# Attention and a Mish feed-forward on one core: the keys' weights turned on TensorE, a shorter warm-up, and a new order of steps

## The chip, the cores and the metric

The kernel runs on one core of a Trainium2 chip. The metric is the time of one execution on the device, in microseconds (us). Three executions of the kernel before took 173.52, 173.74 and 173.78 us; the median is 173.74.

## What is computed

The input x (2048 tokens by 512) is normalised once. Two branches read it: a linear attention of 32 heads of 16, whose features are softmaxes of q and k after a small learned matrix w_phi, and a feed-forward of width 1792 with the Mish function. Their sum is added to x.

```python
def _A_ref(x, wqkv, w_phi, wo):
    qkv = (x @ wqkv).reshape(B, S, 3, H, Dh).transpose(2, 0, 3, 1, 4)
    q, k, v = qkv[0], qkv[1], qkv[2]
    pq = jnp.einsum("bhsd,hdf->bhsf", q, w_phi)
    pk = jnp.einsum("bhsd,hdf->bhsf", k, w_phi)
    phi_q = jnp.concatenate([_softmax(pq), _softmax(-pq)], axis=-1)
    phi_k = jnp.concatenate([_softmax(pk), _softmax(-pk)], axis=-1)
    kv = jnp.einsum("bhsf,bhsd->bhfd", phi_k, v)
    z  = jnp.einsum("bhsf->bhf", phi_k)
    num = jnp.einsum("bhqf,bhfd->bhqd", phi_q, kv)
    den = jnp.einsum("bhqf,bhf->bhq", phi_q, z)[..., None] + 1e-6
    return (num / den).transpose(0, 2, 1, 3).reshape(B, S, D) @ wo

def _B_ref(x, w1, b1, w2):
    h = jnp.einsum("bsd,df->bsf", x, w1) + b1
    return jnp.einsum("bsf,fd->bsd", h * jnp.tanh(softplus(h)), w2)

xn = _layernorm(x)
return x + _A_ref(xn, A_wqkv, A_w_phi, A_wo) + _B_ref(xn, B_w1, B_b1, B_w2)
```

## The kernel before

**Tiles.** The tokens are 16 tiles of 128, in four groups of four. A matrix product over the 512 input columns is four matmuls of 128 rows, one after the other in one PSUM bank. There are six banks of 512 columns, named by @0 to @5 in the list of steps, and a pair of banks (tag "kv") for the attention's sums.

**The order is written out by hand.** `STEPS` (lines 24 to 59) is a string of step names with their arguments; the loop at lines 623 to 625 calls one function for each. Each engine gets its instructions in the order in which the steps are called, and works through them in that order; waits between engines are put in from the data. A number behind @ is the bank that a step writes, and a step that writes a bank waits until the one before it in that bank has been read. The letters v and a at the end say whether VectorE (DVE) or ScalarE (ACT) does a copy or a reciprocal.

**The steps that matter here**, with the functions that they call:

- LS i, RS i, AZ i, TP i, TC i: the first four token tiles. LS takes mean and variance on DVE (lines 545 to 547), RS the inverse root on POOL in two instructions (174 to 177), AZ centres and scales on DVE, TP turns the tile with four transposes on TensorE against an identity, TC copies it from PSUM into `xnT`. LN g and AP g k do the same for the later groups, four tiles at a time, and turn by DMA on the SP queue (line 186).
- F0 kt and FD kt: w_phi is folded into the keys' weights ahead of use. `wT` holds the 512 columns of wqkv for the keys, turned; four matmuls (F0) with the block-diagonal `Wbd` (step WB, from the small load `wsrc`) give 128 rows of the folded weights, and FD copies them into `wkp`. F and FC do so for the queries, later, into the first half of `wqk`; the second half of that tile holds wo.
- LP: the logits of keys for token tiles 0 and 1, eight matmuls that take turns by `kt`. L s i: those of any other tile (s below 4 keys, s from 4 queries). WL 1 and WL 2: two of group 1 into the kv banks. LC copies logits to bf16.
- V t and VC t: values of a tile, and their copy into `vext`.
- H u, M u: 128 of the 1792 hidden columns for one group of tokens, and its Mish on ScalarE with the bias `b1f` (made by PB and CB from `b1b`). O t is the second layer of a tile (14 matmuls of 512 columns), P t adds the attention's output to it (4 matmuls), Y t adds x and stores. The last tile is cut in two, OH, PH and YH.
- E s l: largest (l = 0) or smallest (l = 1) logit of each 16, and the difference, on DVE. X s k: exponentials on ScalarE. S s k: their sums on DVE. R s k and N s k: reciprocal and product for keys; A g k: the sums over tokens on TensorE. W s k: the ratio for queries, and a turn by DMA on SP. KV masks the sums. Q h i, G h i, C h: numerators and denominators on TensorE, their copy from PSUM on ScalarE, and the division with a turn by DMA on SP.

**The start.** Ahead of the steps come the loads. On the SP queue: x_sb of tile 0, then the keys' weights as a turning DMA (`load_turned`, lines 140 to 144), then tiles 2 and 3, wv, half of w1, tiles 4 to 7, the rest of w1. On ScalarE's queue: wsrc, tile 1, b1b. ScalarE then loads the table of the Mish function. POOL makes the identity and the block mask. TensorE meanwhile runs `WARM` = 12 matmuls of ones (lines 511 to 516), whose result nobody reads. ScalarE's functions lie in two tables, one for Mish and one for exponential and logarithm; `table` (134 to 138) loads one when the other is active.

**Buffers.** The sums of exponentials `s` have three buffers, `log`, `r2` and `r` two each (pool `smx`).

Of the kernel before, what the change touches and what calls it, by code (L numbers as in the profile page):

```python
# [29 lines left out]
9; M 10; AP 1 1; H 11 @5; E 0 1; V 4 @1; X 0 1; WL 1; LN 2; V 6 @4; VC 4 a; X 0 0; L 1 0 @2; L 1 3  # L30
@0; LC 1 0 a; V 5 @3; LN 3; VC 5 a; H 12 @1; WL 2; H 13 @2; VC 6 a; S 0 0; LC 1 3 a; M 11; V 3 @3; M
12; M 13; H 14 @4; H 15 @0; H 16 @5; H 17 @1; VC 3 a; M 14; H 18 @2; M 15; M 16; M 17; LC 1 2 a; H
19 @3; AP 2 0; AP 2 1; AP 3 0; L 2 0 @4; LC 2 0 a; L 2 1 @0; LC 2 1 a; V 2 @5; S 0 1; L 2 2 @1; M
18; LC 1 1 a; M 19; H 20 @4; LC 2 2 a; AP 3 1; H 21 @0; WT; H 22 @2; M 20; VC 2 a; R 0 1 v; L 2 3
@3; H 23 @1; R 0 0 v; N 0 1; M 21; N 0 0; H 24 @4; M 22; LC 2 3 a; F 0 @5; F 1 @0; E 1 0; E 1 1; M
23; M 24; F 2 @2; E 2 0; E 2 1; FC 0 a; H 25 @3; H 26 @1; FC 1 a; H 27 @4; M 25; M 26; L 3 2 @5; FC
2 a; M 27; V 7 @0; L 3 3 @3; V 11 @1; F 3 @2; L 3 0 @4; LC 3 0 v; LC 3 2 a; L 3 1 @5; A 0 0; X 1 0;
X 1 1; A 0 1; LC 3 3 a; FC 3 v; S 1 0; V 8 @4; LC 3 1 a; VC 7 a; L 4 0 @2; E 3 0; VC 8 a; LC 4 0 a;
L 4 1 @3; LC 4 1 a; L 4 3 @5; VC 11 a; L 4 2 @0; X 2 0; V 9 @4; L 5 0 @2; H 28 @3; H 29 @1; VC 9 a;
LC 4 2 v; M 28; M 29; H 30 @0; H 31 @4; H 32 @3; M 30; H 33 @1; H 34 @0; M 31; M 32; M 33; M 34; H  # L40
35 @4; M 35; H 36 @3; M 36; S 1 1; LC 4 3 a; R 1 0 v; E 3 1; LC 5 0 a; N 1 0; R 1 1 v; H 37 @1; H 38
@0; H 39 @4; H 40 @3; H 41 @5; H 42 @2; S 2 0; A 1 0; M 37; N 1 1; M 38; M 39; M 40; A 1 1; M 41; M
42; X 3 0; L 6 3 @1; L 5 2 @0; V 10 @4; VC 10 a; L 5 1 @3; LC 5 2 a; L 6 0 @5; E 4 0; E 4 1; X 2 1;
S 3 0; V 15 @2; VC 15 a; V 13 @4; VC 13 a; LC 6 0 a; R 2 0 a; S 2 1; DW 3; R 3 0 a; X 3 1; L 6 1 @0;
LC 5 1 a; DW 2; N 3 0; N 2 0; L 5 3 @2; O 0 @4; S 3 1; V 12 @5; V 14 @3; LC 6 1 a; LC 5 3 a; O 1 @0;
L 6 2 @2; R 2 1 a; N 2 1; VC 14 a; LC 6 3 a; VC 12 v; R 3 1 a; N 3 1; X 4 0; A 2 0; S 4 0; LC 6 2 a;
A 2 1; A 3 0; W 4 0 v; X 4 1; H 43 @3; M 43; A 3 1; H 44 @1; H 45 @5; M 44; H 46 @2; M 45; H 47 @3;
M 46; M 47; H 48 @1; KV; H 49 @5; H 50 @2; Q 0 0; M 48; M 49; G 0 0; M 50; H 51 @3; H 52 @1; H 53
@5; S 4 1; W 4 1 v; M 51; M 52; H 54 @2; H 55 @3; Q 0 1; M 53; E 5 0; E 5 1; M 54; E 6 0; L 7 0 @1;
M 55; G 0 1; C 0 a; X 5 0; LC 7 0 a; L 7 1 @5; X 5 1; O 2 @2; O 3 @3; LC 7 1 a; L 7 2 @1; LC 7 2 a;  # L50
S 5 0; Q 1 0; L 7 3 @5; G 1 0; E 6 1; W 5 0 a; P 0; P 1; Y 0; Q 1 1; O 4 @1; G 1 1; LC 7 3 a; O 5
@4; S 5 1; Q 2 0; O 6 @5; C 1 a; P 2; G 2 0; W 5 1 v; Y 1; Q 2 1; P 3; O 7 @0; E 7 0; X 6 0; S 6 0;
G 2 1; Q 3 0; C 2 a; G 3 0; Y 2; Y 3; X 6 1; O 8 @2; Q 3 1; W 6 0 v; E 7 1; S 6 1; P 4; P 5; G 3 1;
C 3 a; Q 4 0; X 7 0; Y 4; W 6 1 v; X 7 1; S 7 0; O 9 @3; O 10 @1; G 4 0; Q 4 1; P 6; P 7; G 4 1; Y
5; Y 6; C 4 a; Q 5 0; W 7 0 a; G 5 0; O 11 @4; Q 5 1; Y 7; O 12 @5; S 7 1; G 5 1; C 5 a; Q 6 0; G 6
0; O 13 @0; Q 6 1; G 6 1; W 7 1 v; P 8; P 9; Q 7 0; C 6 a; G 7 0; P 10; P 11; Y 8; Q 7 1; G 7 1; O
14 @2; Y 9; Y 10; C 7 a; P 12; P 13; OH 0 @3; PH 0; Y 11; P 14; OH 1 @1; PH 1; Y 12; Y 13; YH 0; Y
14; YH 1
"""
# [3 lines left out]
def kernel(  # L63
# [76 lines left out]
    def load_turned(base_col):  # L140

        wT = lnp.tile([P, 4, 512], BF16, name="wT", tag="xn")
        nc.sync.dma_start_transpose(out=wT[:], in_=A_wqkv[:, base_col : base_col + D])
        return wT

# [343 lines left out]
    nc.sync.dma_start(x_sb[:, 2:4, :], x_v[:, 2:4, :])  # L489
# [67 lines left out]
    def first_turn(i, b):  # L557
        ptr = pf_of["t", i] = bank(b, "ptr", BF16)
        for kt in range(KT):
            nc.tensor.transpose(  # L560
                ptr[:, kt * P : (kt + 1) * P], xn_of[0][:, i, kt * P : (kt + 1) * P], ident[:]
            )
# [93 lines left out]
```

## Time and profile before

| What | Value |
|---|---|
| median of three runs | 173.74 us |
| the profiled execution, its own time | 174.0 us |
| its span, first to last instruction | 172.3 us |
| TensorE busy | 168.7 us, 98% |
| VectorE busy | 143.2 us, 83% |
| ScalarE busy | 119.5 us, 69% |
| table loads on ScalarE | 8, 1.283 us each |
| bytes moved by DMA | 18.02 MB |
| granted TensorE clock, mean | 1.000 |

The span is measured inside the profile, and the time of an execution holds a little more than it. Busy time is the time in which an engine has at least one instruction under way. The profile's engine names are PE for TensorE's matmuls, PEld for its weight loads, DVE for VectorE, ACT for ScalarE, POOL for GpSimd and SP for the queue that issues most DMAs; a q behind a name (SPq, ACTq) stands for instructions that issue DMAs. In the timeline a line has the start, the duration, the engine, the line of the kernel, the operation, output and inputs, a count, and in brackets the idle time before it with what ended it. In the chain of waits a line has the start, the duration and what ran.

### The profile page before, as it was taken

Reading aid. Unit: us, or ns where it says so; the run is one execution under the profiler, and the core shown is the slowest. Engines: PE = TensorE matmul, PEld = TensorE weight load, DVE = VectorE, ACT = ScalarE, POOL = GpSimd, SP = SyncE. Lnnn points to the kernel's source line nnn. Section 1 sums busy time; section 2 is a strip of 40 time slices with the busy share of each in tenths; the row PEclk is TensorE's granted clock in tenths of the full one; section 3 lists DMA queues with packets and bytes.
Section 4 is the critical chain, followed back from the end, with each engine's and each line's share of the span. In section 5 each row is a group of like instructions: output and inputs, shape, how many; then the busy total and the mean of one; then the engine's idle time right before and its main releaser. Section 6 shows DMA issues by size and latency. Waiting matters only on the chain.

```text
span 172.3 us, 2713 instructions
## 1 busy us (share of the span) xinstructions
PE 168.7 (98%) x1039; PEld 82.4 (48%) x1039; DVE 143.2 (83%) x221; ACT 119.5 (69%) x192; POOL 9.4 (5%) x26
## 2 busy tenths in 40 slices
PE   8999999999999999999999999999999999999993
PEld 2554444444545444454446544444444545445452
DVE  2878998999997999979999999799988996844433
...
GB/s 98 269 377 365 82 98 0 37 189 207 366 120 0 0 4 0 0 0 0 4 0 0 64 118 66 12 51 67 150 152 93 150 95 144 172 168 100 173 134 61
DMA packets 44953, 18.02 MB, mean 105 GB/s; under 512 B 37004, under 2 KB 44940, under 8 KB 44940
## 3 DMA queue, kind: packets, MB, share of 16 engines
...
q14 instruction: 5, 0.04, 0.1%
...
## 4 chain that ended last, share of the span: by engine, by line
PE 95%; DMA 3%; SPq 0%; DVE 0%; issue 0%
PE po L463 28%; PE ph L228 28%; PE pl L194 14%; PE po L470 8%; PE pv L194 8%; DMA wT<-in_A_wqkv_dram 3%; PE pnd L418 2%; PE pkv L387 2%; PE pfold L156 1%; PE pwide L194 1%; PE pl L209 1%; PE ptr L560 0%; SPq L483 0%; DVE x_sb L477 0%; PE pb L533 0%
## 5 line engine op out<-in xcount | busy, mean ns | idle before, releaser
L463 PE MATMUL po<-w_sb,acts 128*128 128x512 bf16 (+2 forms) x238 | 50.7, 366 | 0.0
L228 PE MATMUL ph<-xnT,w_sb 128*128 128x512 bf16 x224 | 50.1, 379 | 0.0
L239 ACT ACTIVATE acts<-ph,b1f 128x512 bf16<-128x512 f32 x56 | 37.2, 694 | 4.6 <-PE ph L228 4.4
L305 DVE TENSOR_REDUCE s<-e 128x128 f32<-128x2048 bf16 x16 | 36.4, 2279 | 2.5 <-ACT e L288 2.5
L228 PEld LDWEIGHTS <-w_sb 128*128 128x128 bf16 x224 | 21.7, 98 | 25.5
L463 PEld LDWEIGHTS <-acts 128*128 128x128 bf16 x238 | 22.3, 98 | 24.1
L288 ACT ACTIVATE e<-e 128x2048 bf16<-128x2048 bf16 x16 | 30.3, 1908 | 0.0
L194 PEld LDWEIGHTS <-xnT 128*128 128x128 bf16 x184 | 17.6, 98 | 20.1 <-DMA wv<-in_A_wqkv_dram 0.2
L252 ACT CAST p_sb<-pl 128x512 bf16<-128x512 f32 x27 | 15.4, 587 | 5.5 <-PE pl L194 4.7
L433 ACT COPY ds<-pnd 128x32 f32<-128x32 f32 x16 | 2.9, 183 | 23.5 <-PE pnd L418 23.5
L194 PE MATMUL pv<-wv,xnT 128*128 128x512 bf16 x64 | 16.1, 379 | 0.0
L477 DVE TENSOR_TENSOR x_sb<-po,x_sb 128x512 bf16<-128x512 f32 (+2 forms) x17 | 10.9, 654 | 5.7 <-PE po L470 5.7
L470 PE MATMUL po<-wqk,xnT 128*128 128x512 bf16 (+2 forms) x68 | 15.5, 366 | 0.0
L194 PE MATMUL pl<-wqk,xnT 128*128 128x512 bf16 x64 | 15.3, 379 | 0.0
L170 DVE BATCH_NORM_STATS2 stats<-x_sb 128x6 f32<-128x512 bf16 x16 | 10.1, 679 | 4.3 <-DMA x_sb<-in_A_x_dram 4.3
L263 DVE TENSOR_TENSOR m<-m 128x512 bf16<-128x512 bf16 (+1 forms) x32 | 11.5, 358 | 1.1
L194 PE MATMUL pl<-wkp,xnT 128*128 128x512 bf16 x48 | 11.7, 379 | 0.0
L263 DVE TENSOR_TENSOR m<-p_sb 128x1024 bf16<-128x1024 bf16 x16 | 10.9, 682 | 0.2 <-ACT p_sb L252 0.2
L272 DVE TENSOR_TENSOR e<-p_sb,m 128x2048 bf16<-128x2048 bf16 x8 | 9.8, 1226 | 1.4 <-PE pkv L387 1.1
L272 DVE TENSOR_TENSOR e<-m,p_sb 128x2048 bf16<-128x2048 bf16 x8 | 9.8, 1225 | 0.3
L340 DVE TENSOR_TENSOR e<-e,r 128x2048 bf16<-128x2048 bf16 x8 | 9.6, 1215 | 0.0
L138 ACT ACT_TABLE_LOAD x7 | 9.0, 1283 | 0.1
...
## 6 DMA issues: line engine op xcount, KB each, us to landing
...
```

Source lines behind the costliest of these rows:

```text
L170: nc.vector.bn_stats(stats[:, i, :], xs[:, i, :])
L194: nc.tensor.matmul(pp, lhsT=xnT[:, t, kt, :], rhs=w[:, kt, :], start=(kt == 0), stop=(kt == KT - 1),)
L228: nc.tensor.matmul(ph_of[u][:], lhsT=w1_sb[:, kt, f * P : (f + 1) * P], rhs=xnT[:, g * TPG : (g + 1) * TPG, kt, :], start=(kt == 0), stop= ...
L239: nc.scalar.activation(acts[:, f, g * 512 : (g + 1) * 512], ph_of.pop(u)[:], ACT.Mish, bias=b1f[:, f : f + 1])
L252: copy(p_of[s][:, i, :], pl_of.pop((s, i)))
L263: nc.vector.tensor_tensor(out=m[:], in0=src[:, :, 0:half], in1=src[:, :, half : 2 * half], op=op)
L272: nc.vector.tensor_tensor(out=e_of[s][:].rearrange("p t j l c -> p (t j) l c")[:, :, pl, :].rearrange("p t (c e o) -> p t c e o", e=8, o=2 ...
L288: nc.scalar.activation(v, v, ACT.Exp)
L305: nc.vector.reduce_sum(t[:], pair(s, k).rearrange("p t j l (c e) -> p (t j l c) e", e=16), axis=AX.X)
L463: nc.tensor.matmul(po_of[t, c.stop][:, c], lhsT=acts[:, f, t * P : (t + 1) * P], rhs=w2_sb[:, f, c], start=(f == 0), stop=False,)
L470: nc.tensor.matmul(po_of[t, c.stop][:, c], lhsT=oT_of[t // 2][:, t % 2 * 4 + j, :], rhs=wo_sb[:, j, c], start=False, stop=(j == 3),)
L477: nc.vector.tensor_tensor(out=y, in0=po_of.pop((t, c.stop))[:, c], in1=y, op=ALU.add)
```

## The change

1. The keys' weights are loaded as they lie in memory, in two halves, into `wkp` itself; the turning DMA is gone for the keys and stays for the queries. New steps TW 0 to 3 turn them with four plain matmuls each against the identity, and TK 0 to 3 copy the result from PSUM into `wT`, all on ScalarE. FD then writes the folded weights over the loaded ones in `wkp`.
2. `WARM` is 9.
3. The root of token tile 1 is made on ScalarE with a logarithm and an exponential (RS 1 a); tiles 0, 2 and 3 stay on POOL. ScalarE starts with the table that has both; a new step TM loads the Mish table ahead of the first Mish.
4. The sums `s` have six buffers, `r2` three, `r` one; the logarithm is written over its input and `log` is gone.
5. b1b is loaded on SP behind the first half of w1. wo is asked for at the start (DW 3), ahead of the six turns of xn. w2 comes in two pieces in place of three.
6. The list of steps is in a new order, with some copies and reciprocals on the other engine.

```diff
-WARM = 12
+WARM = 9
...
-LS 0; RS 0; DX 2; LS 1; WB; RS 1; AZ 0; TP 0 @0; F0 0 @1; F0 1 @2; AZ 1; FD 0 v; TP 1 @3; TC 1 v; LS
-2; PB @4; RS 2; TC 0 a; LS 3; RS 3; FD 1 a; AZ 2; F0 2 @5; F0 3 @0; FD 2 a; FD 3 a; LP i @1,2; KM;
-DX 3; AZ 3; V 0 @3; LC 0 0 a; TP 2 @5; V 1 @0; TC 2 a; TP 3 @1; VC 0 a; LC 0 1 v; TC 3 v; CB; L 0 2
-@5; L 0 3 @2; LC 0 3 a; LN 1; H 0 @3; H 1 @1; H 2 @4; M 0; LC 0 2 a; H 3 @2; M 1; M 2; M 3; VC 1 a;
...
+TW 0 @0; TW 1 @1; TW 2 @2; DX 2; LS 0; RS 0 p; LS 1; RS 1 a; TW 3 @3; WB; DX 3; TK 0 a; AZ 0; AZ 1;
+TP 0 @4; LS 2; TK 1 a; F0 0 @5; TK 2 a; RS 2 p; TC 0 v; TP 1 @0; TC 1 v; FD 0 a; AZ 2; TK 3 a; LS 3;
+F0 1 @1; F0 2 @2; FD 2 a; DW 3; V 0 @4; FD 1 a; F0 3 @0; RS 3 p; TP 2 @5; TC 2 v; FD 3 a; LP i @3,2;
+KM; AZ 3; PB @1; CB; TP 3 @5; TC 3 v; LC 0 0 a; L 0 2 @0; LC 0 2 a; LC 0 1 a; L 0 3 @1; LC 0 3 a; LN
+1; E 0 0; AP 1 0; AP 1 1; TM; H 0 @3; LN 2; E 0 1; H 1 @5; H 2 @0; M 0; H 3 @2; H 4 @1; H 5 @3; M 1;
...
+L 1 0 @4; H 12 @0; H 13 @2; M 9; M 10; L 1 3 @1; M 11; H 14 @3; X 0 0; LN 3; H 15 @5; X 0 1; LC 1 0
+v; LC 1 3 a; S 0 1; WL 1; WL 2; M 12; H 16 @4; AP 2 1; M 13; R 0 1 v; M 14; H 17 @1; H 18 @0; H 19
...
-    tables = ["mish"]
+    tables = ["natural_log_exp_and_others"]
...
-        t = s_of[s, k] = smx.tile([P, 128], FP32, name="s", bufs=3)
+        t = s_of[s, k] = smx.tile([P, 128], FP32, name="s", bufs=6)
...
-    def log(src, n):
+    def log(v):
...
-        t = smx.tile([P, 128], FP32, name="log")
-        nc.scalar.activation(t[:, 0:n], src, ACT.Ln)
-        return t[:, 0:n]
+        nc.scalar.activation(v, v, ACT.Ln)
+        return v
...
-        r2 = r_of[s, k] = smx.tile([P, 128, 2], BF16, name="r2")
+        r2 = r_of[s, k] = smx.tile([P, 128, 2], BF16, name="r2", bufs=3)
...
     nc.sync.dma_start(x_sb[:, 0, :], x_v[:, 0, :])
-    wT_of = {0: load_turned(D)}
+    for k in (slice(0, 2), slice(2, 4)):
+        nc.sync.dma_start(wkp[:, k, :], wqkv_v[:, k, D : 2 * D])
+    wT_of = {0: lnp.tile([P, 4, 512], BF16, name="wT", tag="xn")}
...
-    nc.scalar.dma_start(b1b[:], b1_v[:, :])
...
     nc.sync.dma_start(w1_sb[:, :, 0 : 7 * P], w1_v[:, :, 0 : 7 * P])
+    nc.sync.dma_start(b1b[:], b1_v[:, :])
...
-    nc.scalar.preload_act_table_set("mish")
+    nc.scalar.preload_act_table_set("natural_log_exp_and_others")
...
+    nc.vector.memset(eps[:], 1e-5)
...
+    def first_root(i, how):
         _, mv, rstd = ln_of[0]
-        root(rstd[:, i : i + 1], mv[:, i : i + 1, :])
+        if how == "p":
+            root(rstd[:, i : i + 1], mv[:, i : i + 1, :])
+            return
+        table("natural_log_exp_and_others")
+        t = lnp.tile([P, 1], FP32, name="lnvar")
+        nc.scalar.activation(t[:], mv[:, i, 1:2], ACT.Ln, bias=eps[:])
+        nc.scalar.activation(rstd[:, i : i + 1], t[:], ACT.Exp, scale=-0.5)
...
+    def turn_keys(kt, b):
+        ptw = pf_of["w", kt] = bank(b, "ptw")
+        for j in range(4):
+            nc.tensor.matmul(
+                ptw[:, j * P : (j + 1) * P], lhsT=wkp[:, kt, j * P : (j + 1) * P], rhs=ident[:],
+                start=True, stop=True,
+            )
+
+    def keep_keys(kt, copy):
+        copy(
+            wT_of[0][:, :, kt * P : (kt + 1) * P],
+            pf_of.pop(("w", kt))[:].rearrange("p (j c) -> p j c", j=4),
+        )
...
-            for f in (slice(0, 5), slice(5, 10), slice(10, FT)):
+            for f in (slice(0, 7), slice(7, FT)):
...
+        "TM": lambda: table("mish"), "KM": masks, "WB": weights_by_block, "PB": bias,
+        "TW": turn_keys, "TK": lambda kt, c: keep_keys(kt, copies[c]),
```

More of the change, by code (lines that the diff above doesn't have):

```diff
@@ L30 @@
[L30 to L58, printed above, removed]
+TW 0 @0; TW 1 @1; TW 2 @2; DX 2; LS 0; RS 0 p; LS 1; RS 1 a; TW 3 @3; WB; DX 3; TK 0 a; AZ 0; AZ 1;
+TP 0 @4; LS 2; TK 1 a; F0 0 @5; TK 2 a; RS 2 p; TC 0 v; TP 1 @0; TC 1 v; FD 0 a; AZ 2; TK 3 a; LS 3;
@@ new lines @@
+F0 1 @1; F0 2 @2; FD 2 a; DW 3; V 0 @4; FD 1 a; F0 3 @0; RS 3 p; TP 2 @5; TC 2 v; FD 3 a; LP i @3,2;
+KM; AZ 3; PB @1; CB; TP 3 @5; TC 3 v; LC 0 0 a; L 0 2 @0; LC 0 2 a; LC 0 1 a; L 0 3 @1; LC 0 3 a; LN
+1; E 0 0; AP 1 0; AP 1 1; TM; H 0 @3; LN 2; E 0 1; H 1 @5; H 2 @0; M 0; H 3 @2; H 4 @1; H 5 @3; M 1;
+M 2; M 3; M 4; H 6 @5; M 5; M 6; H 7 @0; AP 2 0; H 8 @2; VC 0 a; H 9 @1; M 7; M 8; H 10 @3; H 11 @5;
+L 1 0 @4; H 12 @0; H 13 @2; M 9; M 10; L 1 3 @1; M 11; H 14 @3; X 0 0; LN 3; H 15 @5; X 0 1; LC 1 0
@@ new lines @@
+v; LC 1 3 a; S 0 1; WL 1; WL 2; M 12; H 16 @4; AP 2 1; M 13; R 0 1 v; M 14; H 17 @1; H 18 @0; H 19
+@2; M 15; M 16; M 17; M 18; LC 1 2 a; M 19; H 20 @3; M 20; H 21 @5; M 21; H 22 @4; M 22; AP 3 0; V 2
+@1; VC 2 a; LC 1 1 a; AP 3 1; N 0 1; WT; H 23 @0; H 24 @2; S 0 0; L 2 3 @3; M 23; M 24; H 25 @5; M
+25; H 26 @4; R 0 0 v; H 27 @1; L 2 0 @0; M 26; L 2 1 @2; M 27; LC 2 0 a; LC 2 3 a; F 0 @5; LC 2 1 a;
+L 2 2 @4; LC 2 2 a; E 1 0; E 1 1; FC 0 a; V 3 @1; VC 3 a; H 28 @0; F 1 @3; H 29 @2; H 30 @4; M 28;
@@ new lines @@
+FC 1 a; E 2 0; H 31 @5; E 2 1; M 29; M 30; M 31; F 2 @1; F 3 @0; L 3 1 @3; FC 2 v; V 1 @2; VC 1 v; X
+1 0; L 3 3 @4; X 1 1; V 11 @5; L 3 0 @1; LC 3 0 a; L 3 2 @2; LC 3 1 v; N 0 0; V 8 @3; LC 3 2 v; S 1
+0; LC 3 3 a; A 0 0; S 1 1; A 0 1; FC 3 a; V 6 @1; X 2 0; VC 11 v; V 7 @2; VC 6 a; S 2 0; VC 7 a; R 1
+0 a; N 1 0; V 4 @4; L 4 1 @0; V 10 @1; VC 8 a; VC 10 a; L 4 0 @2; R 1 1 a; VC 4 a; L 4 2 @3; L 4 3
+@5; LC 4 0 a; LC 4 2 v; LC 4 1 a; LC 4 3 a; V 5 @1; VC 5 a; V 12 @4; H 32 @2; H 33 @0; X 2 1; N 1 1;
@@ new lines @@
+H 34 @5; A 1 0; A 1 1; H 35 @3; R 2 0 a; M 32; H 36 @1; M 33; M 34; H 37 @2; M 35; M 36; H 38 @0; H
+39 @5; E 4 0; H 40 @3; VC 12 a; M 37; M 38; M 39; H 41 @1; H 42 @4; DW 2; N 2 0; H 43 @2; E 3 0; E 4
+1; L 6 0 @0; M 40; M 41; M 42; M 43; LC 6 0 a; E 3 1; H 44 @5; M 44; X 3 0; V 15 @3; S 2 1; L 6 1
+@1; L 6 3 @4; V 9 @2; LC 6 3 a; VC 15 v; V 13 @0; O 0 @5; X 4 1; VC 9 a; L 5 2 @3; S 3 0; X 3 1; VC
+13 a; L 5 0 @4; V 14 @2; LC 5 0 a; LC 5 2 a; S 4 1; R 3 0 a; A 2 0; L 6 2 @0; LC 6 2 a; S 3 1; H 45
@@ new lines @@
+@4; L 5 3 @3; N 3 0; R 2 1 a; N 2 1; R 3 1 a; N 3 1; O 1 @0; A 2 1; A 3 0; LC 5 3 a; X 4 0; S 4 0; L
+5 1 @3; VC 14 a; LC 6 1 a; M 45; LC 5 1 a; A 3 1; W 4 0 v; KV; H 46 @2; H 47 @1; M 46; H 48 @4; M
+47; H 49 @3; H 50 @2; H 51 @1; M 48; M 49; H 52 @4; M 50; M 51; H 53 @3; W 4 1 v; E 5 0; E 5 1; Q 0
+0; M 52; M 53; H 54 @2; H 55 @1; G 0 0; Q 0 1; M 54; M 55; G 0 1; E 6 0; X 5 0; L 7 3 @4; L 7 0 @3;
+LC 7 0 a; S 5 0; Q 1 0; LC 7 3 a; L 7 2 @2; O 2 @1; O 3 @3; G 1 0; Q 1 1; C 0 a; O 4 @4; W 5 0 v; P
@@ new lines @@
+0; P 1; E 6 1; G 1 1; C 1 a; LC 7 2 a; Y 0; X 5 1; S 5 1; Y 1; Q 2 0; G 2 0; L 7 1 @2; O 5 @5; LC 7
+1 a; W 5 1 v; X 6 0; S 6 0; E 7 0; Q 2 1; P 2; W 6 0 v; P 3; Y 2; Y 3; O 6 @2; G 2 1; Q 3 0; C 2 a;
+O 7 @0; X 6 1; G 3 0; S 6 1; Q 3 1; G 3 1; C 3 a; W 6 1 a; O 8 @1; E 7 1; Q 4 0; O 9 @3; G 4 0; Q 4
+1; G 4 1; P 4; P 5; P 6; Y 4; P 7; Y 5; Q 5 0; C 4 a; X 7 0; O 10 @4; S 7 0; G 5 0; X 7 1; Y 6; W 7
+0 v; S 7 1; Y 7; Q 5 1; O 11 @5; G 5 1; C 5 a; O 12 @2; Q 6 0; G 6 0; P 8; W 7 1 v; Y 8; P 9; Y 9; Q
@@ L59 @@
+6 1; O 13 @0; G 6 1; C 6 v; Q 7 0; P 10; Y 10; G 7 0; P 11; Q 7 1; O 14 @1; G 7 1; C 7 v; OH 0 @3; Y
+11; P 12; Y 12; P 13; P 14; Y 13; Y 14; PH 0; OH 1 @4; PH 1; YH 0; YH 1
 """
@@ L123 @@
     mhalf = consts.tile([P, TPG], FP32, name="mhalf")
+    eps = consts.tile([P, 1], FP32, name="eps")
     block = consts.tile([P, 8, 16], BF16, name="block")
@@ L138, in table @@
             nc.scalar.preload_act_table_set(name)
[L140 to L144, printed above, removed]
     def bank(b, name, dtype=FP32):
@@ L316, in power @@
         )
-    def log(src, n):
+    def log(v):
         table("natural_log_exp_and_others")
-        t = smx.tile([P, 128], FP32, name="log")
-        nc.scalar.activation(t[:, 0:n], src, ACT.Ln)
-        return t[:, 0:n]
+        nc.scalar.activation(v, v, ACT.Ln)
+        return v
     def invert(s, k, how):
         t = s_of.pop((s, k))
-        r2 = r_of[s, k] = smx.tile([P, 128, 2], BF16, name="r2")
+        r2 = r_of[s, k] = smx.tile([P, 128, 2], BF16, name="r2", bufs=3)
         if how == "a":
-            power(r2[:], log(t[:], 128), 128, -1.0)
+            power(r2[:], log(t[:]), 128, -1.0)
             return
-        r = smx.tile([P, 128], BF16, name="r")
+        r = smx.tile([P, 128], BF16, name="r", bufs=1)
         with nc.allow_low_precision("the softmaxes are bf16"):
@@ L350, in weigh @@
         if how == "a":
-            t4 = log(t[:], 128).rearrange("p (t l c) -> p t l c", l=2, c=4)
+            t4 = log(t[:]).rearrange("p (t l c) -> p t l c", l=2, c=4)
             nc.vector.tensor_tensor(
@@ L446, in combine @@
         if how == "a":
-            power(f[:], log(d, 64), 64, -1.0)
+            power(f[:], log(d), 64, -1.0)
         else:
@@ L600, in load_queries @@
     def load_queries():
-        wT_of[1] = load_turned(0)
+        wT_of[1] = lnp.tile([P, 4, 512], BF16, name="wT", tag="xn")
+        nc.sync.dma_start_transpose(out=wT_of[1][:], in_=A_wqkv[:, 0:D])
     run = {
-        "KM": masks, "WB": weights_by_block, "PB": bias,
+        "TM": lambda: table("mish"), "KM": masks, "WB": weights_by_block, "PB": bias,
         "CB": lambda: nc.vector.tensor_copy(b1f[:], pf_of.pop("b")[:, 0:FT]),
         "LS": first_stats, "RS": first_root, "AZ": first_apply, "TP": first_turn,
+        "TW": turn_keys, "TK": lambda kt, c: keep_keys(kt, copies[c]),
         "LP": first_logits, "TC": lambda i, c: first_keep(i, copies[c]),
```

2 lines of the change are left out of this document (removed).

## The prediction

> **What bounds the kernel now.** I read the page's busy shares first, then the chain of waits in order of time, then the timeline of the first 14 us.
>
> ```profile
> PE 168.7 (98%) x1039; PEld 82.4 (48%) x1039; DVE 143.2 (83%) x221; ACT 119.5 (69%) x192; POOL 9.4 (5%) x26
> ```
>
> ```profile
> 1.25 5.36 DMA wT<-in_A_wqkv_dram
> 6.61 0.05 issue
> 6.65 0.62 PE pfold L156 x8
> ...
> 8.16 1.73 PE pl L209 x8
> 9.88 0.86 PE pv L194 x4
> ...
> 169.41 0.24 PE po L470 x4
> 169.65 0.02 issue
> 169.67 0.29 DVE x_sb L477
> ```
>
> From 6.65 to 169.65 us the chain is TensorE and nothing else, and the pieces run at the rate of the large matmuls (four of 512 columns in 0.86, so 0.216 each). No other engine holds it up. Ahead of it stand 5.4 us for the turned load of the keys' weights (wT). So a version that never starves TensorE can gain only ahead of 6.65 us, and it ends earlier by as much as the same remaining matmuls start earlier.
>
> ```profile
> 0.83 5.28 PE L513 MATMUL warm<-const-bfloat16-1.0 128*128 128x512 bf16 x12 [0.83 <-PEq L640]
> 1.25 3.12 SPq L143 DMA_TRANSPOSE wT<-in_A_wqkv_dram  x1
> 4.41 0.69 DVE L170 BATCH_NORM_STATS2 stats<-x_sb 128x6 f32<-128x512 bf16 x1 [0.32 <-DMA x_sb<-in_A_x_dram]
> 4.42 0.56 SPq L489 DMA_DIRECT2D x_sb<-in_A_x_dram  x1
> 6.03 0.53 PE L560 MATMUL ptr<-ident,xn 128*128 128x128 bf16 x4
> 7.31 1.74 ACT L165 CAST wkp<-pfold 128x512 bf16<-128x512 f32 x3
> 9.72 1.03 PE L194 MATMUL pv<-wv,xnT 128*128 128x512 bf16 x4
> ```
>
> The warm-ups take 0.427 us each (starts 0.83, 1.25, 1.68 and so on to 5.53), twice 0.216; the eight folds at 6.65 run at full speed (0.45 us of weight loads). SP is held 3.12 us by the turned load, so x_sb of tokens 2 and 3 is not asked for before 4.42. The first logits (LP) issue from 8.00 to 9.72; all after them is without a gap.
>
> **The mark to beat.** At the end of LP the new order has already done V 0 (0.86) and TP 2 (0.22), and has not done PB (0.11). The same work is left when its LP ends at 9.72+0.86+0.22-0.11 = 10.69 us. In the new order V 0, F0 3, TP 2 and LP follow each other: 0.86+0.22+0.22+1.73 = 3.03. So V 0 must start by 7.66 us to break even.
>
> **The loads.** The turned load and its 3.12 us on SP go; two plain loads of 256 KB follow x_sb 0. Landings by a rate: wv was used at 9.54, the first part of w1 landed at 5.54+6.4 = 11.94 (the shortest landing among w_sb's), so 917 KB took 2.40 us, 382 GB/s. x_sb 0 lands at 3.18 as now. From there at 382: token tile 1, wsrc and the first half of the weights (0.40 MB) 4.2, second half 4.9, tokens 2 and 3 5.6, wv 6.9, w1 9.3, b1b just behind it 9.4 (PB wants it at 10.6), tokens 4 to 7 10.7 (DVE wants them after TC 3, at 11.6). At 200 GB/s, which is what 1.5 to 7.5 us moved with the turned load in it (1.2 MB), wv would land at 10; at 300 at 8.0. I take 382, as these are plain loads like the measured ones. The load of wo goes onto SP ahead of the six xnT transposes; it and all loads are over by 3.18+5.4 MB/382 = 17 us, and the first such transpose is ready at 19, so it hides; w2 in two pieces in place of three is on SP by 45 and wanted at 83.
>
> **Nine warm-ups** end at 0.83+9*0.427 = 4.67 instead of 5.95. The 16 turning matmuls (TW) of 128 columns take 16*0.107 = 1.71 at the warm-ups' speed, until 6.4, or 0.9 at full speed; both ends hide, since what follows needs ScalarE.
>
> **The chain on ScalarE** decides V 0. Token 1's root moves there from POOL, so ScalarE, which works in order, waits for token 1's moments before the first TK copy; behind it stand all eight TK and FD copies. Token 1 landed at 4.41; without the turned load I take 4.25 (4.09, the end of DVE's work on token 0, to 4.8 if the 512 KB push it back). Moments 0.91 (4.41 to 5.32), hand-over 0.09. Ln and Exp on one column are not in the trace: a 32-column copy takes 0.18, Ln of 128 columns 0.32; the line through Ln's rows (269 ns at 64, 315 at 128) gives 0.22 and Exp's 0.20. So the root is there at 4.25+0.91+0.09+0.22+0.03+0.20 = 5.70. The copies step by 0.48 where their data waits (three logits copies at 86.44 take 1.54, the last 0.58); alone 0.587. TK 0 to 2 then end at 5.70+0.48+0.48+0.59 = 7.25, and F0 2 runs from 7.30 to 7.52. Beside it DVE: Wbd, centring 0 and 1 until 6.16, moments of token 2 until 6.95, TC 0 (0.42) until 7.3. V 0 needs F0 2's turn, TC 0 and wv (6.9): it starts at 7.52, LP ends at 10.55, **0.14 us ahead** of the mark. The early end (4.09) gives V 0 at 7.36 and 0.3 gained; the late ends (4.8, copies 0.587) 8.28 and 0.6 lost. FD 0, TK 3, FD 2, FD 1 and FD 3 follow in steps of 0.48 until 9.7, each ahead of its part of LP.
>
> **The body.** TensorE's remaining work is the same. DVE gets two TC (0.42 each), two VC (0.69), two C (0.70), a W (0.62) and an LC (0.69), and loses an FD (0.69) and two R (1.24): 1.8 us more. ScalarE gets four TK and an FD (0.59 each), two R (0.73), the root (0.42) and a table load (TM, 1.28), and loses two TC, two VC and an LC (0.59), two C (0.58) and a W (0.62): 1.4 more. Both had room (83 and 69%), so the sums cost nothing unless the order starves TensorE. Two tight places. (1) From LP's end PB, TP 3, two L (2.06 together) and twelve H (10.37) bring H 11's end to 23.0; M 11 ends at 23.9, then a table load, X 0 0, X 0 1 (1.82+1.89), one copy (0.48), a table load and M 12 (0.69): 31.4. TensorE does ten groups after H 11 (8.64) and wants bank 0 back for H 18 at 31.6. Slack 0.2. (2) H 55 ends at 105.9 by the same counting; M 55, G 0 1, a table load, X 5 0, S 5 0 (2.2), C 0 (0.7) and W 5 0 (1.4) end at 115.0; C 0's transpose (1.23) is off SP by then, and W 5 0's lands 3.2 after its issue: 118.2, against Q 2 0 at 120.1. Six sum buffers instead of three take waits away and add none; in-place logarithms cost the same rows; three r2 and one r likewise.
>
> **The end.** P 14 is first to need C 7 in place of PH 0; 7.0 us of matmuls stand behind Q 7 1 in both (O 14 3.02, OH 0 2.28, two P 1.73). Copies 0.8, C 7 on DVE 1.5, transpose 3.3 and hand-overs make 6.0. Same tail.
>
> **Sum.** Span 172.3-0.14 = 172.2; the profiled run took 174.0, 1.7 around the span, so 173.9; it lay 0.26 above the median of 173.74. On the median, 173.6; since the early end of token 1's landing seems the nearer one (no turned load beside it) I round down: **173.5 us**.
>
> **The rivals.**
> - *Full speed comes late* (slower). Full speed came in this trace only after 5.3 us of warm-ups. If the second half of the weights lands later than TW 1's end (4.67+0.85 = 5.5), TensorE has holes where it had work; if the 5.3 us count anew from there, half speed lasts to 10.8: V 0 costs 0.86 more, F0 3 and TP 2 0.44, and LP, from 9.7 to 10.8 at half speed, 0.55. 1.85 lost on 173.5: 175.3. Against it: TW at half speed itself fills 4.67 to 6.4, as long as the twelve warm-ups and ptr did, and the 0.28 us gap at 6.37 did no harm. It decides from a landing after 5.5. The Trainium skill (TensorE: Matmul & The Clock Gate, Part 1) says that a free-running window of about 3.4 us must be busy before the clock doubles; by that rule full speed at 6.1 to 6.6 came from a window that opened near 3, though no row here shows the window itself; a miss would keep half speed to about 9.8 and cost some 1.3, an estimate from that page.
> - *A starved body* (slower): at H 18, if ScalarE is 0.2 late. TensorE waits for M 12 and takes the lag to the end. ScalarE late by the second table load or by the slower copies is worth 0.3 to 1.2: 174.4. For it: slack 0.2 there; against: ScalarE's mish step by 0.62 in a row (four in 2.47), so behind M 12 it gains 0.24 on each H.
> - *Late loads*: wv at 8.0 (300 GB/s) puts V 0 at 8.1: 0.4 lost, 174.1; at 200, 2.5 lost. For it: 90 to 290 GB/s up to 5 us; against: those were the turned load and 32-byte rows.
> - *The head gains more* (faster): token 1 at 4.09 and Ln and Exp at 0.10 each put the root at 5.32, V 0 at 7.14, 0.5 gained: 173.2. For it: one column only; against: 0.18 is the shortest row on ScalarE.
>
> **How the numbers follow.** Chances: forecast 0.55 (own range 173.3 to 174.2), clock 0.12, body 0.15, loads 0.10, head 0.08. About 0.2% (0.35 us, so below 173.39 and above 174.09) is what can be told from no change. The forecast's share splits 0.21 faster, 0.29 same, 0.05 slower; with head faster, clock slower, body 0.12 slower and 0.03 same, loads 0.06 slower and 0.04 same: 0.29, 0.36, 0.35. The range takes in head, loads at 300, body at its dearest (174.7) and nearly the clock: 172.9 to 175.1; out are loads at 200 and the clock's full price.
>
> **What would show it.** LP's last matmul issued near 10.5; ScalarE's first TK copy at 5.6 to 5.9 just behind an Exp; F0, V 0 in a row from 7.2; folds and ptr at 0.22 per four; no wait of TensorE after LP, in the waits' view, above 0.1. Wrong would be: V 0 waiting for wv; weight loads of TensorE 0.1 apart after 6.6; a wait of PE for ScalarE at H 18.

## The result, and the profile after

Six executions of the changed kernel took 174.39 to 174.87 us, median 174.71; six of the kernel before beside them 173.52 to 173.95, median 173.76. The ratio is 1.0048, 95% interval 1.0038 to 1.0059: slower by 0.95 us at the medians, where 173.5 had been forecast. The profiled execution took 174.72 with a span of 173.0; that of before, 174.0 and 172.3, lay 0.24 above its own median. A ratio leaves out executions that are over 1.5% longer than the fastest of their kernel; below, that is so for two of e13 alone.

The busy shares of after, its chain of waits in order of time (start, duration, what ran), and where H 0 stands in the chain of before:

```profile
PE 169.3 (98%) x1052; PEld 83.7 (48%) x1052; DVE 145.4 (84%) x227; ACT 120.9 (70%) x193; POOL 8.9 (5%) x24
```

```profile
2.73 5.42 DMA wv<-in_A_wqkv_dram
8.15 0.14 issue
8.29 1.02 PE pv L189 x4
...
9.76 1.73 PE pl L204 x8
...
13.65 10.36 PE ph L223 x48
...
170.39 0.02 issue
```

```profile
13.78 10.36 PE ph L228 x48
```

TensorE's share is unchanged; the 0.6 us more are the 16 turning matmuls (1.89) less three warm-ups (5.28 - 4.00 = 1.28). The chain no longer begins with the turned keys' weights but with wv, which ends at 8.15, and is TensorE alone from 8.29 on. From H 0 (13.65) to TensorE's end (170.39) there are 156.74 us. Before, it was 13.78 to 169.65, 155.87, with V 1 (0.86) still ahead of H 0. So behind H 0 the two kernels do the same work in the same time, and the whole difference of the two profiled executions is ahead of it: 13.65 + 0.86 - 13.78 = 0.73 us.

That is 0.73 of the 0.95 at the medians. The other 0.2 belongs to before's profiled execution, which was a long one. The run e7 below has the same start as before, and its profiled execution took 173.77; there H 0 starts 0.21 sooner:

```profile
13.57 10.36 PE ph L228 x48
```

The timeline of after there (start, duration, engine, line, operation, output and inputs, count, and the idle time before it with what ended it):

```profile
4.72 0.69 DVE L165 BATCH_NORM_STATS2 stats<-x_sb 128x6 f32<-128x512 bf16 x1 [0.85 <-DMA x_sb<-in_A_x_dram]
4.73 1.62 PEld L572 LDWEIGHTS <-wkp 128*128 128x128 bf16 x16 [0.81 <-DMA wkp<-in_A_wqkv_dram]
...
5.67 0.29 ACT L555 ACTIVATE lnvar<-mv,eps 128x1 f32<-128x1 f32 x1 [2.55 <-DVE mv L167]
...
6.10 1.54 ACT L578 CAST wT<-ptw 128x512 bf16<-128x512 f32 x3
...
7.38 0.72 DVE L584 COPY xnT<-ptr 128x512 bf16<-128x512 bf16 x2
...
7.69 0.23 PEld L151 LDWEIGHTS <-wT 128*128 128x128 bf16 x4 [0.25 <-ACT wT L578]
...
8.26 0.56 PEld L189 LDWEIGHTS <-xnT 128*128 128x128 bf16 x4 [0.34 <-DVE xnT L584]
8.29 1.02 PE L189 MATMUL pv<-wv,xnT 128*128 128x512 bf16 x4 [0.20 <-DMA wv<-in_A_wqkv_dram]
...
9.60 1.89 PE L204 MATMUL pl<-wkp,xnT 128*128 128x512 bf16 x8
```

Tile 1 is used at 4.72 (before: 4.41), so ScalarE's root starts at 5.67, three copies of the turned weights end at 7.64, and the third fold, whose weight loads wait for ScalarE at 7.69, is through at 7.92. V 0 needs that fold's turn on TensorE, the first half of xnT (DVE, 7.38 to 7.77) and wv (8.15). It was to start by 7.66 to break even and starts at 8.29; LP issues from 9.60 for 1.73, to 11.33, against a mark of 10.69: 0.64 late, and PB follows 0.09 behind. Together that is the 0.73 above. Of the 0.64, wv's landing makes 0.37 (7.92 to 8.29) and ScalarE's chain 0.26 (7.66 to 7.92).

The transfers' rate by half microseconds (after; stretch, length, busy times, granted clock, DMA share, GB/s), the issue of wv (KB, us to landing), and the place where before waits for wv:

```profile
1.50:2.00 0.50, 0.50 (x2) 0.15 (x1) 0.00 (x0) 0.17 (x1) 0.36 (x3) 1.00 0.16 55
...
2.50:3.00 0.50, 0.50 (x3) 0.23 (x2) 0.04 (x1) 0.50 (x1) 0.05 (x1) 1.00 0.95 156
...
4.00:4.50 0.50, 0.50 (x2) 0.00 (x0) 0.00 (x0) 0.00 (x0) 0.42 (x2) 1.00 1.09 379
...
5.50:6.00 0.50, 0.50 (x8) 0.50 (x6) 0.50 (x3) 0.30 (x2) 0.00 (x0) 1.00 1.12 248
```

```profile
wv<-in_A_wqkv_dram SPq DMA_DIRECT2D x1, 512.0 KB, 5.4
```

```profile
9.54 0.71 PEld L194 LDWEIGHTS <-xnT 128*128 128x128 bf16 x4 [0.15 <-DMA wv<-in_A_wqkv_dram]
```

The last number of a row is the rate. Summed over all rows of the view, 1.95 MB had moved by 8.15, though only 1.59 MB were asked for up to and with wv (tile 0 and tile 1 131 KB each, keys' weights 524, wsrc 16, tiles 2 and 3 262, wv 524). So 0.36 MB asked for behind wv moved before wv counted as landed: about 1.1 us at the 340 GB/s of 3.18 to 8.15 (1.69 MB in 4.97 us). The trace's single packets say what these bytes were. A packet of w1 has 1792 bytes and one of wv 1024, the lengths of their rows. The first packet of w1 starts at 6.67, the last of wv ends at 7.80, and 0.20 MB of w1 have moved by then. Another 0.35 us pass between the last packet of wv and its landing at 8.15; in before they are 0.38 (9.12 to 9.50). Before, wv was asked for at 5.04 and used at 9.54: issued 2.31 us earlier, it was there only about 1.4 earlier.

The Trainium skill (DMA: Bandwidth & Descriptors, Why a DMA increments its semaphore by 16 and not by 1) says that a DMA runs on up to 16 engines that finish independently, and that only the full count means that all of its data has landed. Packets of w1 ahead of the last ones of wv agree with that; which engine carried a packet the trace does not show.

### The profile page after: what moved, and what is told of

It reads as the page before. It is cut to its first block, busy times and chain, and to the rows that moved or that the text cites. A ratio compares the mean times of both kernels' runs of the same rounds, so it can differ in the third digit from the quotient of the medians.

```text
span 173.0 us, 2746 instructions
## 1 busy us (share of the span) xinstructions
PE 169.3 (98%) x1052; PEld 83.7 (48%) x1052; DVE 145.4 (84%) x227; ACT 120.9 (70%) x193; POOL 8.9 (5%) x24
## 4 chain that ended last, share of the span: by engine, by line
PE 94%; DMA 3%; SPq 1%; issue 0%; DVE 0%
PE po L457 28%; PE ph L223 28%; PE pl L189 14%; PE pv L189 8%; PE po L464 8%; DMA wv<-in_A_wqkv_dram 3%; PE pnd L412 2%; PE pkv L381 2%; PE pwide L189 1%; PE pl L204 1%; PE pfold L151 1%; SPq L481 1%; PE ptr L565 0%; SPq L486 0%; SPq L477 0%
## 5 line engine op out<-in xcount | busy, mean ns | idle before, releaser
L234 ACT ACTIVATE acts<-ph,b1f 128x512 bf16<-128x512 f32 x56 | 36.5, 702 | 5.1 <-PE ph L223 4.9
L247 ACT CAST p_sb<-pl 128x512 bf16<-128x512 f32 x26 | 14.2, 584 | 3.6 <-PE pl L189 2.4
L464 PE MATMUL po<-wqk,xnT 128*128 128x512 bf16 (+2 forms) x68 | 15.0, 366 | 0.0
```

The source lines that it names most:

```text
L234: nc.scalar.activation(acts[:, f, g * 512 : (g + 1) * 512], ph_of.pop(u)[:], ACT.Mish, bias=b1f[:, f : f + 1])
L247: copy(p_of[s][:, i, :], pl_of.pop((s, i)))
L464: nc.tensor.matmul(po_of[t, c.stop][:, c], lhsT=oT_of[t // 2][:, t % 2 * 4 + j, :], rhs=wo_sb[:, j, c], start=False, stop=(j == 3),)
```

## The experiments

"Before" stands for the kernel before on the same chip in the same session, at 173.76 to 173.99.

**Is it wv, or tile 1?** Two edits of loads in the changed kernel, and both together (e4_halves_tile1).

```diff
 # e1_wv_halves
-    nc.sync.dma_start(wv[:], wqkv_v[:, :, 2 * D : 3 * D])
+    for k in (slice(0, 2), slice(2, 4)):
+        nc.sync.dma_start(wv[:, k, :], wqkv_v[:, k, 2 * D : 3 * D])
 # e2_tile1_first
+    nc.scalar.dma_start(x_sb[:, 1, :], x_v[:, 1, :])
         nc.scalar.dma_start(wsrc[:], wphi_v)
-    nc.scalar.dma_start(x_sb[:, 1, :], x_v[:, 1, :])
```

> The changed kernel with the load of wv cut in two halves by rows (kt 0 and 1, kt 2 and 3). Theory A, the loss is V 0's late start, 0.36 us of it the wait for wv (landing 8.15, while F0 2 was through at 7.92): the first half lands near 7.5, V 0 starts at 7.9, LP's last matmul is issued near 11.0 in place of 11.33, median near 174.35. Theory B, ScalarE's row of TK and FD copies alone sets LP: LP waits for FD 3 instead, median stays at 174.7.

> The changed kernel with token tile 1 loaded ahead of wsrc on ScalarE's queue. Tile 1 should land near 4.25 in place of 4.72, the root near 5.7, the TK copies 0.45 earlier. Theory A (wv's landing is the last thing V 0 waits for): at most 0.1 gained, 174.6. Theory B (ScalarE's chain from token 1's moments sets V 0): 0.4 gained, 174.3.

> Both edits on the loads together: wv in halves and token tile 1 ahead of wsrc. Theory A with ScalarE's chain as the next wait behind wv: the two add up, V 0 at 7.55, LP's end 10.6 to 10.7, median 174.0 to 174.1. If the chain does not matter at all: as wv in halves alone, 174.35.

Measured: e1 174.89 us (ratio 1.0055, 1.0039 to 1.0071), e2 174.85 (1.0057, 1.0044 to 1.007), e4 174.99 (1.0062, 1.0046 to 1.0078). None gained. The timelines of e1, then e2, say why:

```profile
6.04 1.54 ACT L579 CAST wT<-ptw 128x512 bf16<-128x512 f32 x3
...
7.63 0.23 PEld L151 LDWEIGHTS <-wT 128*128 128x128 bf16 x4 [0.26 <-ACT wT L579]
...
7.87 1.03 PE L189 MATMUL pv<-wv,xnT 128*128 128x512 bf16 x4
```

```profile
4.24 0.66 DVE L165 BATCH_NORM_STATS2 stats<-x_sb 128x6 f32<-128x512 bf16 x1
...
5.59 1.54 ACT L578 CAST wT<-ptw 128x512 bf16<-128x512 f32 x3
...
8.63 1.02 PE L189 MATMUL pv<-wv,xnT 128*128 128x512 bf16 x4 [0.68 <-DMA wv<-in_A_wqkv_dram]
```

In e1 V 0 no longer waits for wv, but for the third fold, and that for ScalarE's copy: 0.42 earlier than after's, still past 7.66; and over six executions (174.49, the profiled one and the shortest, to 175.15) nothing is left of it. In e2 the root's chain is 0.5 earlier, and wv lands 0.34 later (8.49). In e4 V 0 waits at 8.11 for DVE, whose moments of tile 2 waited for a load until 6.83. So V 0 stands behind several arrivals that are all late, and taking one away uncovers the next.

**Is it the root on ScalarE, ahead of the copies?** RS 1 p in place of RS 1 a in the changed kernel.

```diff
-LS 1; RS 1 a; TW 3 @3; WB; ...
+LS 1; RS 1 p; TW 3 @3; WB; ...
```

> The changed kernel with token 1's root on POOL again (RS 1 p), so that ScalarE starts the TK copies as soon as TW 0 is through, near 5.3 in place of 6.1. Theory A: V 0 still waits for wv, and DVE's centring of token 1, and TC 0 behind it, come 0.4 later: 174.7 to 174.9. Theory B: 0.6 gained, 174.1.

Measured: 175.15 (1.0075, 1.0057 to 1.0093). The copies start 0.8 earlier than in after, and V 0 starts 0.47 later (timeline of e3, and its issue of wv):

```profile
5.29 1.56 ACT L578 CAST wT<-ptw 128x512 bf16<-128x512 f32 x3 [2.17 <-PE ptw L572]
...
6.81 0.41 DVE L176 TENSOR_SCALAR xn<-x_sb,mv,rstd 128x512 bf16<-128x512 bf16 x1 [0.47 <-POOL rstd L172]
...
8.76 1.02 PE L189 MATMUL pv<-wv,xnT 128*128 128x512 bf16 x4 [0.64 <-DVE xnT L584]
```

```profile
wv<-in_A_wqkv_dram SPq DMA_DIRECT2D x1, 512.0 KB, 5.9
```

With POOL's root the second centring starts at 6.81 (in after two centrings in a row end at 6.65). Behind it in DVE's order stand the moments of tile 2 and only then the first half of xnT, which ends at 8.43 in place of 7.77. The timeline puts V 0's wait down to DVE, but wv was later still: issued at 2.73 as in after, it landed at 8.62 in place of 8.15. So V 0 waited for wv here too, and what DVE's delay alone would cost is not shown. Nothing was gained by copies that start earlier, because they were not the last arrival.

**Is it the nine warm-ups?** Twelve in the changed kernel; nine in the kernel before.

> The changed kernel with twelve warm-up matmuls. Theory A: TW starts at 5.95 in place of 4.73 and the first TK copy 0.4 later, V 0 near 8.4: 174.8 to 174.9. Theory C, nine warm-ups leave TensorE at half speed where it matters: 174.0 or less.

> The kernel before with nine warm-ups and nothing else changed. TensorE then stands still from 4.67 to 6.03. If this leaves the speed as it is: 173.8. If full speed needs the unbroken stretch of 5.3 us: half speed in the folds and LP, 0.5 to 1.9 lost, 174.3 to 175.6.

Measured: e5 175.16 (1.0075, 1.0049 to 1.0101): twelve give nothing back. Three of its executions took 174.5 to 174.85, about as after, and three 175.47 to 176.02. In the profiled one (175.47) the loads came late: tile 1 was used at 5.33 and wv landed 6.0 us after its issue. e6 174.19 (1.0034, 1.0009 to 1.006) falls into two groups: seven executions at 173.72 to 174.27, five at 175.07 to 175.64. The timeline of a dear one, 175.35:

```profile
5.79 0.34 PEld L560 LDWEIGHTS <-xn 128*128 128x128 bf16 x4 [1.88 <-DVE xn L181]
...
6.45 1.03 PE L156 MATMUL pfold<-Wbd,wT 128*128 128x128 bf16 x8
...
8.79 2.39 PE L209 MATMUL pl<-wkp,xnT 128*128 128x512 bf16 x8
```

Eight folds take 1.03 us in place of 0.62, LP 2.39 in place of 1.89: half speed until about 9.8. The granted clock of the profile reads 1.00 all the while, but it reads 1.00 for the warm-ups of before too, which ran at half speed: where the trace has no clock record the view counts full speed. The first record of full speed stands at 9.79 in this trace, at 6.36 in that of before. TensorE had a hole from about 4.7 to 5.79. In the changed kernel the turning matmuls fill it (4.73 to 6.35), and full speed is recorded from 6.72.

The Trainium skill (TensorE: Matmul & The Clock Gate, Part 1) says that full speed follows a busy window of about 3.4 us, and that this window is free-running, so that it does not start with the kernel. Two groups 1.5 us apart agree with that: in the dear one, by that rule, a window was spoilt by the hole and the next one had to pass. A stretch at half speed of 3.41 us, in e13 below, agrees too.

**Is it the body?** Buffers and in-place logarithms alone in the kernel before (e7); then the new order and buffers behind the kernel before's own start (e8, e10; wo's load early, V 1 and its copy ahead of H 0 as in before; b1b's and w2's loads as in before). These two start with Mish's table like before, so that TM loads nothing in them: they have 8 table loads, after has 9.

```diff
 # e10_old_head2: STEPS of before up to CB, then those of after behind TP 3
 LS 0; RS 0; DX 2; LS 1; WB; RS 1; AZ 0; TP 0 @0; ... TP 3 @1; VC 0 a; LC 0 1 v; TC 3 v; CB;
+VC 1 a; L 0 2 @5; L 0 3 @2; LC 0 2 a; LC 0 3 a; LN 1; E 0 0; AP 1 0; AP 1 1; TM; H 0 @3; LN 2; ...
```

> The kernel before with the buffers of the change alone (s six, r2 three, r one, the logarithm in place). TensorE has no gap after 8 us that they could fill: 173.8, no change.

> The steps of the kernel before up to CB, with its loads and twelve warm-ups, and the new order of steps with the new buffers behind them (V 1 stays early). Theory A (the whole loss lies ahead of the first hidden layer): 173.7 to 173.9, and no wait of TensorE after LP. Theory D (the new order of the rest costs part of it): 174.2 to 174.7.

> As e8_old_head, with the banks chosen so that no logits wait for VC 1 (L 0 2 into bank 5, L 0 3 into bank 2, banks 1 and 5 exchanged in the steps behind). Old loads, turned keys' weights, twelve warm-ups and the old steps up to CB; new order and new buffers behind them. Theory A (the whole loss lies in the new head): 173.7 to 173.9, H 0 at 13.6 to 13.8 and no wait of TensorE behind it. Theory D (the new order behind the head costs part of the loss): 174.2 or more.

Measured: e7 173.81 (0.9999, 0.9991 to 1.0008). e8 174.59 (1.0041, 1.0028 to 1.0054), by a flaw of its own: L 0 2 was put into V 1's bank and waited 0.6 for its copy. e10, with other banks, 173.85 (1.0008, 0.9996 to 1.002). Its chain:

```profile
1.25 5.20 DMA wT<-in_A_wqkv_dram
6.44 0.05 issue
6.49 0.62 PE pfold L155 x8
...
8.00 1.73 PE pl L208 x8
...
13.62 10.36 PE ph L227 x48
```

The new order behind the start and its buffers cost at most 0.35 us (the interval's end, 1.002), and nothing that can be told. The ninth table load is not in e10; after's own chain, TensorE alone from 8.29 on, shows that it costs nothing there. So the loss is in the new start.

**Can the new start be mended?** e11: tile 1 first, wv in halves ahead of tiles 2 and 3, the root on POOL, moments of tiles 2 and 3 behind the second xnT copy, tiles 2 and 3's transposes behind LP.

> The changed kernel with all three waits ahead of V 0 taken away together: token tile 1 ahead of wsrc; wv in halves and ahead of tiles 2 and 3; token 1's root on POOL; moments of tiles 2 and 3 behind TC 1; TP 2 behind LP, V 0's copy and V 1 early as a filling behind LP. Theory A (three waits stand close together, each hides the others): V 0 near 7.4, LP's end near 10.2, H 0 near 13.4, median 173.3 to 173.7. Rival (the turn on TensorE with its copies is slower than the turning load whatever the order, or the landings spread too far): 173.9 to 174.5.

Measured: 174.99 (1.0085, 1.0055 to 1.0115; 174.53 to 176.47). V 0 started at 7.97 in the profiled execution, the earliest but e1's, and yet late:

```profile
6.06 0.62 PE L573 MATMUL ptw<-ident,wkp 128*128 128x128 bf16 x8 [0.38 <-DMA wkp<-in_A_wqkv_dram]
...
7.97 1.03 PE L189 MATMUL pv<-wv,xnT 128*128 128x512 bf16 x4
```

The second half of the weights, unturned, came at 6.06. Behind LP, TensorE then waited for the centring that the moved transposes need, and H 0 started at 14.31 (before: 13.78, with V 1 ahead of it in both).

**What does the route alone cost?** The kernel before with plain loads, TW and TK and nine warm-ups, all else as it was (e12); the same with tile 1 ahead of wsrc (e14); that with the root on ScalarE between the copies (e15).

```diff
-    wT_of = {0: load_turned(D)}
+    for k in (slice(0, 2), slice(2, 4)):
+        nc.sync.dma_start(wkp[:, k, :], wqkv_v[:, k, D : 2 * D])
+    wT_of = {0: lnp.tile([P, 4, 512], BF16, name="wT", tag="xn")}
...
-LS 0; RS 0; DX 2; LS 1; WB; RS 1; AZ 0; TP 0 @0; F0 0 @1; ...
+LS 0; RS 0; DX 2; LS 1; WB; RS 1; TW 0 @1; TW 1 @2; TK 0 a; TK 1 a; TW 2 @4; TW 3 @5; TK 2 a; TK 3 a; AZ 0; TP 0 @0; F0 0 @1; ...
```

> The kernel before with the route of the keys' weights alone changed: two plain loads of 256 KB, four turning steps on TensorE, four copies on ScalarE, nine warm-ups; roots on POOL, V 0 behind LP, tables, buffers and the rest of the order as before. Theory (the route itself is no earlier than the turned load: second half landed at 4.9 to 6.05 in the runs so far, then four copies by 0.48 and the fold, so LP ends 0.3 to 1 us later than before's 9.72): 174.2 to 174.9. Rival (the route is good, and what costs is only V 0 ahead of LP with the root on ScalarE ahead of the copies; LP then ends at 9.7 to 9.9): 173.5 to 174.0.

> As the kernel before with the plain route alone, and token tile 1 asked for first on ScalarE's queue, wsrc behind it. There tile 1 landed at 4.86, 0.45 later than in the kernel before, and DVE's chain from it (moments, centring, second transpose at 7.37 against 7.11) put the first logits at 8.26 against 8.00. If that landing is the whole price of the route, tile 1 is used at 4.2 to 4.4, logits start at 7.9 to 8.05 and the time is 173.7 to 174.1. If what tile 1 gains the keys' weights or wsrc lose (the plain second half landed at 5.87 when tile 1 went first), logits start at 8.2 or later: 174.2 to 174.8.

> The same with the root of tile 1 on ScalarE, behind the second of the four copies, and the table for it loaded first, Mish's behind the first values' copy. If a root on ScalarE helps where the copies stand ahead of it: second transpose 0.3 to 0.5 earlier, logits from 7.6 to 7.8: 173.3 to 173.8. If it only delays copies 3 and 4 of the turned weights, or the second table load delays the first Mish: 173.9 to 174.6.

Measured: e12 174.29 (1.0033, 1.0011 to 1.0055; eleven executions at 174.21 to 174.92, one at 176.61), e14 174.56 (1.0036, 1.0024 to 1.0049), e15 174.75 (1.0052, 1.0039 to 1.0066). The timelines of before, e12 and e14:

```profile
7.11 0.39 PE L560 MATMUL ptr<-ident,xn 128*128 128x128 bf16 x4
...
8.00 1.89 PE L209 MATMUL pl<-wkp,xnT 128*128 128x512 bf16 x8
```

```profile
4.86 0.69 DVE L170 BATCH_NORM_STATS2 stats<-x_sb 128x6 f32<-128x512 bf16 x1 [0.75 <-DMA x_sb<-in_A_x_dram]
...
5.66 0.62 PE L569 MATMUL ptw<-ident,wkp 128*128 128x128 bf16 x8 [0.45 <-DMA wkp<-in_A_wqkv_dram]
...
7.37 0.40 PE L562 MATMUL ptr<-ident,xn 128*128 128x128 bf16 x4
...
8.26 1.89 PE L209 MATMUL pl<-wkp,xnT 128*128 128x512 bf16 x7
```

```profile
6.15 0.62 PE L569 MATMUL ptw<-ident,wkp 128*128 128x128 bf16 x8 [0.72 <-DMA wkp<-in_A_wqkv_dram]
...
6.58 1.07 ACT L575 CAST wT<-ptw 128x512 bf16<-128x512 f32 x2 [0.27 <-PE ptw L569]
...
7.77 0.81 PE L156 MATMUL pfold<-Wbd,wT 128*128 128x128 bf16 x8
...
8.42 1.94 PE L209 MATMUL pl<-wkp,xnT 128*128 128x512 bf16 x8
```

In e12 tile 1 comes 0.45 later than before, by DVE the second transpose 0.26 later (7.37 against 7.11), and LP 0.26 later (8.26 against 8.00). With tile 1 asked for first (e14), nothing is gained: DVE takes tile 1 at 4.86 as in e12, because now tile 0 comes at 4.03 (3.20 in e12). The second half of the weights comes 0.49 later than in e12, its two copies end at 7.65, the last folds start at 7.77 (7.54 before), and LP starts at 8.42. The rival held, as far as one profiled execution of each can show. From its landing (6.15) to the fold that needs it (7.77) the route takes 1.6 us. The unturned second half was used at 5.43 to 6.58 in the eight profiled executions where TensorE waited for it; the turned load went straight into the folds when it landed, at 6.36 to 6.65 in the five that have it on SP behind tile 0. The root on ScalarE with its table load (e15 against e14) adds 0.2 at the medians and in the profiles (LP at 8.61 against 8.42), but the two intervals overlap.

**Can the old start be better?** The kernel before with its turned load first on SP and tile 0 moved to ScalarE's queue, tile 1 and wsrc behind it.

```diff
-    nc.sync.dma_start(x_sb[:, 0, :], x_v[:, 0, :])
+    nc.scalar.dma_start(x_sb[:, 0, :], x_v[:, 0, :])
...
+    nc.scalar.dma_start(x_sb[:, 1, :], x_v[:, 1, :])
         nc.scalar.dma_start(wsrc[:], wphi_v)
-    nc.scalar.dma_start(x_sb[:, 1, :], x_v[:, 1, :])
```

> The kernel before with its turned load first on the SP queue; token tile 0 goes first on ScalarE's queue, tile 1 behind it. If the start of the folds hangs on the landing of the turned load (it landed at 6.61, issued at 1.25), it is issued some 0.45 us earlier, folds start near 6.2 and the time is 173.2 to 173.5. If its landing doesn't move, or tile 0 or tile 1 now land later and transposes and logits wait for them, 173.7 to 174.3.

Measured: 175.49 to 176.74 in four executions (their ratio 1.0126, 1.0098 to 1.0154), 178.23 and 178.63 in two: far past both. Timeline, and the page's line of the granted clock in 40 slices of 4.4 us:

```profile
5.87 0.69 DVE L170 BATCH_NORM_STATS2 stats<-x_sb 128x6 f32<-128x512 bf16 x1 [1.59 <-DMA x_sb<-in_A_x_dram]
...
7.04 0.43 DVE L524 TENSOR_TENSOR Wbd<-block,wsrc 128x512 bf16<-128x512 bf16 x1 [0.27 <-DMA wsrc<-in_A_w_phi_dram]
...
7.85 0.61 PE L560 MATMUL ptr<-ident,xn 128*128 128x128 bf16 x4 [2.76 <-DVE xn L181]
```

```profile
PEclk9879999999999999999999999999999999999999
```

Tile 1 came at 5.87 and the 16 KB of wsrc at 6.95; TensorE stood 2.8 us. Behind that hole the trace's clock records show half speed from 7.32 to 10.73, 3.41 us long. The execution with a mean granted clock of 1.00 took 175.49, the three with 0.989 took 176.35 to 176.74, the two with 0.981 the 178 us. So the late loads alone cost 1.5, and half speed goes with 0.9 to 3.1 more. No version tried beats the kernel before.

## Why the prediction was wrong

**The step that failed is the loads.** "From there at 382 ... wv 6.9" measured 8.15, and tile 1 "I take 4.25" measured 4.72. Both rest on one idea: without the turned load, the start moves bytes at the rate of the later plain loads, one load after the other. The rate was 55 to 276 GB/s up to 3.5 us and 340 on average from 3.18 to 8.15, and bytes of the next load moved before wv was in. The prediction's own terms (1.46 MB from 3.18 at 382) give 6.99 for wv, not 6.9. By 3.18, 0.26 MB had moved and not 0.13 (worth 0.34 us); the lower rate costs 0.43, and w1's 0.36 MB 1.06: 6.99 - 0.34 + 0.43 + 1.06 = 8.14. V 0 waiting for wv, which the trace shows, was the prediction's own sign of being wrong.

**The rounding down** to 173.5, because token 1 would come sooner with no turned load beside it, went the wrong way by the same step. With wsrc ahead of it, tile 1 was used at 3.98 to 4.41 in the five profiled executions with the turned load, and at 4.66 to 5.33 in the five with two plain loads of 256 KB in its place (after, e1, e3, e5, e12).

**The sum.** From 173.5 to 174.71 are 1.2 us: the rounding 0.1, LP's end 0.78 (10.55 forecast, 11.33 measured), PB's 0.09, and 0.24 that had been taken off because before's profiled execution lay above its median. After's profiled execution lay on its own.

**Late loads** was the right rival, at 0.10 too small a chance. It put V 0 at 8.1 for wv at 8.0; measured 8.29 for 8.15. Its 174.1 counts the 0.4 from V 0's break-even of 7.66 on the old median; the later landing (0.2), PB's 0.09 and the 0.24 bring it to 174.6.

**The chain on ScalarE** was right but for its start. From the first ScalarE instruction (5.67) to the first copy it took 0.43 (0.45 forecast), from there to the end of TK 2 1.54 (1.55). Its 0.40 of lateness (F0 2 at 7.92, not 7.52) is tile 1's landing: 0.47 late, less 0.07 that the steps behind it were shorter.

**That V 0 goes ahead of LP** was counted as free. It is not a cost in work, but it makes three arrivals meet at the first place where TensorE can stop: the third fold, xnT and wv. In before, wv was wanted only behind LP, at 9.5. The single edits do not share out the loss between V 0's place and ScalarE's root: e12's 0.30 at the medians is the route's with its nine warm-ups, e14 to e15 about 0.2, not clear of noise, the root's where it stands between the copies. What V 0's place adds by itself was not run, so its share stays open.

**Right:** the mark and the break-even of 7.66; nine warm-ups with the turning matmuls behind them ("until 6.4": 6.35); no late full speed in the profiled execution, though e6 shows that the danger is there (1.5 us in five of twelve; 1.3 and 1.85 were the estimates, and the 5.3 us of warm-ups from which the second counted were one case among several, see the last section); the body, free at H 18 and Q 2 0; the tail (span less TensorE's end is 2.6 in both). Before's span of 172.3 and the 0.64 and 0.09 make 173.0, as measured.

**Luck:** that the range of 172.9 to 175.1 holds 174.71 is owed to the prices of the body and the clock, which did not come; the forecast's own range ended at 174.2. The late end of the ScalarE chain, V 0 at 8.28, is near the measured 8.29 by chance: there the copies were to be last, and wv was.
